# Table signs by memset, one filter copy and one evacuation moved to ScalarE, in the opening of an FFT filter + MLP kernel

## The chip, the cores and the metric

One core of a Trainium2 chip. The metric is device microseconds of one execution. A profiled execution leaves a trace; its "span" is 1.8 us shorter than the device time of the same execution (770.64 against 772.45 in the kernel before). Below, "us N" is an instant of a trace, counted from the start of its span. Instants with two decimals that stand in no fence are single records of a trace.

## The reference, cut to what matters

```python
def _attn_ref(x, filt_r, filt_i):            # x (8, 3008, 256)
    X = np.fft.rfft(x, axis=1)
    Y = X * (filt_r + 1j * filt_i)[None]
    return np.fft.irfft(Y, n=x.shape[1], axis=1)

def _moe_ref(x, w_in, w_out):                # (24064, 256) -> 2048 -> 256
    h = x @ w_in
    g = 0.5 * h * (1.0 + erf(h / sqrt(2)))
    return g @ w_out
```

The transform runs along 3008 = 47 x 64 as matmuls with tables: stage 1 over 47, a transpose, stage 2 over 64, the product with the filter, stages 3 and 4 back. The result of batch 0 feeds the first MLP matmul; from then on the kernel works on the MLP of one batch and the transform of the next side by side.

Of the kernel before, what the change touches and what calls it, by code (L numbers as in the profile page):

```python
# [10 lines left out]
ALU = mybir.AluOpType  # L11
FP32 = mybir.dt.float32
BF16 = mybir.dt.bfloat16
# [4 lines left out]
NA, NB = 47, 64  # L18
# [11 lines left out]
class _Mix:  # L30
# [63 lines left out]
    def dup_filters(self, eng, k0, k):  # L94
        for k in range(k0, k0 + k, 2):
            o, i = (self.F[r:r + 64, :, k:k + 2, :].rearrange("p t a b -> p t (a b)") for r in (64, 0))
            eng.tensor_copy(out=o, in_=i)  # L97

    def gate(self, t):

# [24 lines left out]
    def table_1(self, g):  # L125

        nc, ts = self.nc, self.nc.vector.tensor_scalar
        col = lambda name: g.tile([128, 1], FP32, name=name)
        off = g.tile([128, 2, K1], FP32, name="off")
        nc.vector.memset(off[:, 0, :], 0.25)  # L130
        nc.vector.memset(off[:, 1, :], 0.5)
        h, n1, hs, hc = col("h"), col("n1"), col("hs"), col("hc")
        ts(out=h, in0=self.p, scalar1=float(NA), scalar2=None, op0=ALU.is_ge)
        nc.vector.scalar_tensor_tensor(out=n1, in0=h, scalar=-float(NA), in1=self.p, op0=ALU.mult, op1=ALU.add)
        ts(out=hs, in0=h, scalar1=2.0 * PI, scalar2=None, op0=ALU.mult)
        ts(out=n1, in0=n1, scalar1=1.0 / NA, scalar2=None, op0=ALU.mult)
        ts(out=hc, in0=h, scalar1=-2.0 * PI, scalar2=2.0 * PI, op0=ALU.mult, op1=ALU.add)
        self.turn_signs(g)
        self.weights_4(g)
        w, r = g.tile([128, 2, K1], FP32, name="w1"), g.tile([128, 2, K1], FP32, name="r1")  # L140
        nc.vector.scalar_tensor_tensor(out=w, in0=self.k48, scalar=n1, in1=off, op0=ALU.mult, op1=ALU.add)
        ts(out=r, in0=w, scalar1=RND, scalar2=-RND, op0=ALU.add, op1=ALU.add)
        nc.vector.tensor_tensor(out=w, in0=w, in1=r, op=ALU.subtract)
        for q, s in enumerate((hc, hs)):
            nc.scalar.activation(out=self.T1[:, 48 * q:48 * q + 48], in_=w[0:2 * NA].rearrange("p a b -> p (a b)"),
                                 func=AF.Sin, scale=s[0:2 * NA])
# [16 lines left out]
    def table_2_angle(self, g, h):  # L163


        v = self.nc.vector
        ts = v.tensor_scalar
        w = self.gen[:, 0]
        if h == 0:
            col = lambda name: g.tile([128, 1], FP32, name=name)  # L170
            jn = g.tile([128, NB], FP32, name="jn")
            ts(out=jn, in0=self.jj, scalar1=self.n2, scalar2=self.ri, op0=ALU.mult, op1=ALU.add)
            n6, self.n12 = col("n6"), col("n12")
            ts(out=n6, in0=self.n2, scalar1=6.0, scalar2=None, op0=ALU.mult)
            ts(out=self.n12, in0=self.n2, scalar1=12.0, scalar2=None, op0=ALU.mult)
            v.scalar_tensor_tensor(out=w[:, 0:6], in0=self.kk.unsqueeze(2).to_broadcast([128, 6, NB]), scalar=self.n2,
                                   in1=jn.unsqueeze(1).to_broadcast([128, 6, NB]), op0=ALU.mult, op1=ALU.add)
            ts(out=w[:, 6:12], in0=w[:, 0:6], scalar1=n6, scalar2=None, op0=ALU.add)
        else:
            ts(out=w[:, 12:24], in0=w[:, 0:12], scalar1=self.n12, scalar2=None, op0=ALU.add)  # L180
        k = slice(12 * h, 12 * h + 12)
        ts(out=self.gen[:, 1, k].bitcast(I32), in0=w[:, k].bitcast(I32), scalar1=15, scalar2=None,
           op0=ALU.logical_shift_left)

    def turn_signs(self, g):

        ts = self.nc.vector.tensor_scalar
        q, b = (g.tile([128, 1], FP32, name=n) for n in ("q64", "b32"))
        self.turn = [g.tile([128, 1], FP32, name=n) for n in ("turn_r", "turn_i")]
        ts(out=q, in0=self.p, scalar1=64.0, scalar2=-64.0, op0=ALU.is_ge, op1=ALU.mult)  # L190
        self.nc.vector.tensor_tensor(out=q, in0=self.p, in1=q, op=ALU.add)
        ts(out=b, in0=q, scalar1=32.0, scalar2=2.0, op0=ALU.is_ge, op1=ALU.mult)
        ts(out=self.turn[0], in0=b, scalar1=1.0, scalar2=-1.0, op0=ALU.mult, op1=ALU.add)
        ts(out=self.turn[1], in0=b, scalar1=-1.0, scalar2=1.0, op0=ALU.mult, op1=ALU.add)

    def unit_matrices(self, g, cols):
        ts = self.nc.vector.tensor_scalar
# [13 lines left out]
    def table_2_swap(self, h):  # L211
        t2 = self.T2[:, 12 * h:12 * h + 12]
        for i in range(2):
# [2 lines left out]
                                  start=True, stop=True)  # L216
            self._evac(t2[:, :, 1, 32 * i:32 * i + 32], ps[:, 0:384].rearrange("p (k j) -> p k j", k=12),
                       "act", 1.0 - 2.0 * i)

    def weights_4(self, g):  # L220

        ts = self.nc.vector.tensor_scalar
        q, self.wt, self.wtc = (g.tile([128, 1], FP32, name=n) for n in ("q48", "wt", "wtc"))
        ts(out=q, in0=self.p, scalar1=48.0, scalar2=-48.0, op0=ALU.is_ge, op1=ALU.mult)
        self.nc.vector.tensor_tensor(out=q, in0=self.p, in1=q, op=ALU.add)
        ts(out=self.wt, in0=q, scalar1=2.0, scalar2=1.0, op0=ALU.is_ge, op1=ALU.add)
        ts(out=self.wtc, in0=self.p, scalar1=4.0, scalar2=1.0, op0=ALU.is_ge, op1=ALU.add)


    def table_4(self, t4, t1, wt, tag, eng):  # L230
# [297 lines left out]
def kernel(  # L528
# [9 lines left out]
    m = _Mix(ctx, tc, x, filt_r, filt_i, moe_w_in, moe_w_out, out)  # L538
    nc, B, S = tc.nc, m.B, m.S
# [3 lines left out]
    g = m.small  # L543
    wide = ctx.enter_context(ExitStack())
    m.psum(wide, w=(2, 1), m=(1, 1), n=(5, 1))
    act = "act"
# [7 lines left out]
    for sgn, lo, base in ((1, 0, 0), (-1, 32, m.S - NA)):  # L554
# [5 lines left out]
    m.ones = g.tile([128, 512], BF16, name="ones")  # L560
    nc.vector.memset(m.ones, 1.0)
    m.warm_up(10)
    m.table_1(g)
    m.table_2_rows(g)
    m.T1c = g.tile([2 * NA, 96], BF16, name="T1c")
    nc.vector.tensor_copy(out=m.T1c.rearrange("p (k h r) -> p k h r", h=2, r=2),
                          in_=m.T1.rearrange("p (h r k) -> p k h r", h=2, r=2))
    m.gen = m.py.tile([128, 2, K1, NB], FP32, tag="y", name="gen")
    m.table_2_angle(g, 0)
    m.unit_matrices(g, cols)  # L570
# [11 lines left out]
    for u in range(16):  # L582
# [12 lines left out]
        if u == 11:  # L595
# [2 lines left out]
            m.table_3_turn(0)  # L598
            m.warm_up(1)
    m.table_3(1)  # L600
    m.table_3_copy(1, False)
    m.dup_filters(nc.vector, 0, 4)
    m.warm_up(1)
    m.c1t(0, (False, False))
    m.c1t(1, (act,))
# [29 lines left out]
    m.load_x(1)  # L635
    m.load_w_out(0)
    m.load_w_out(8)

    warm = g.tile([128, 1], FP32, name="warm")
    nc.scalar.activation(out=warm, in_=m.p, func=AF.Gelu)  # L640
# [3 lines left out]
    for u in range(10):  # L644
        if u < 8:
            m.c3t(u)
        if u >= 2:
            m.c4(u - 2, (act, False if u > 7 else act))
    wide.close()
    m.psum(ctx, h=(3, 1), o=(2, 1), f=(3, 1))  # L650

# [29 lines left out]
    for s in range((NT + 1) * 16):  # L681
        t, jc = s // 16, s % 16
# [37 lines left out]
```

## The kernel before: the parts that the change touches

All of the change lies in "the opening": tables and the transform of batch 0, before the first MLP matmul.

```python
def dup_filters(self, eng, k0, k):           # second half of a filter tile: partitions 0..63 -> 64..127
    for k in range(k0, k0 + k, 2):
        o, i = (self.F[r:r + 64, :, k:k + 2, :].rearrange("p t a b -> p t (a b)") for r in (64, 0))
        eng.tensor_copy(out=o, in_=i)        # 64x1024, bf16

def table_3_turn(self, q):                   # two bf16 copies with a sign per partition, SBUF to SBUF
    k = slice(8 * q, 8 * q + 8)
    for r in range(2):
        self.nc.vector.tensor_scalar(out=self.T3i[:, k, r, :], in0=self.T3[:, k, 1 - r, :],
                                     scalar1=self.turn[r], scalar2=None, op0=ALU.mult)

def c2(self, p):                             # stage 2, and the product with the filter
    ...                                      # two matmuls into ps
    nc.vector.tensor_tensor(out=w, in0=ps.unsqueeze(1).to_broadcast([128, 2, 512]),
                            in1=f.rearrange("p t a b -> p t (a b)"), op=ALU.mult)
...
# ---- the body (cut) ----
m.table_1(g)
m.table_2_rows(g)
...
m.table_2_angle(g, 0)                        # begins with turn_signs and weights_4: nine 128x1 operations
...
for k, n in ((0, 4), (4, 8), (12, 12)):
    m.load_filters(k, n)                     # three groups of transfers, issued by Pool
m.load_w_in()
...
m.dup_filters(nc.gpsimd, 4, 20)              # ten copies on Pool
m.table_2_sin(0)
for u in range(16):
    m.c1(...)                                # stage 1; every four need another piece of x
    ...
m.table_3(1)
m.table_3_copy(1, False)                     # ScalarE
m.dup_filters(nc.vector, 0, 4)               # two copies on VectorE
m.warm_up(1)
m.c1t(0, (False, False))                     # transposes, evacuated to b_sb by VectorE
m.c1t(1, (act,))
m.c2(0)                                      # first product
m.table_3_turn(1)
m.warm_up(1)
m.c2(1)                                      # second product
...
for q in range(1, 7):
    if q < 6:
        m.c2(2 * q); ...; m.c2(2 * q + 1)    # third to twelfth product
    ...                                      # stage 3
for u in range(10):
    if u < 8:
        m.c3t(u)
    if u >= 2:
        m.c4(u - 2, (act, False if u > 7 else act))   # stage 4; False is VectorE
```

## Time and profile before

| | before |
|---|---|
| time, three runs | 772.91 us (772.91 to 772.94) |
| span of the profiled run | 770.64 us |
| first MLP matmul | 38.76 us |
| from there to the end of the span | 731.88 us |

The prediction below shows the lines of this profile and reads them.

### The profile page before, as it was taken

What the parts mean: (1) busy time and instruction counts of PE and PEld (TensorE: products, weight loads), DVE (VectorE), ACT (ScalarE), POOL (GpSimd) and SP (SyncE); (2) the same over time, 40 slices, a digit from 0 to 9 for tenths busy, and PEclk for the clock granted to TensorE, in tenths of its full rate; (3) what the DMA queues carried; (4) which work ended last, traced back from release to release, by engine and by line L of the source; (5) the groups of instructions that cost most, each with busy time, mean ns of one, the idle gap of its engine ahead of it and who ended that gap; (6) DMA issues with size and microseconds to landing.
All of it is one profiled execution on the core that took longest, in us unless ns stands there. A gap on an engine that the chain in (4) does not pass through costs nothing.

```text
span 770.6 us, 15044 instructions
## 1 busy us (share of the span) xinstructions
PE 763.5 (99%) x6057; PEld 527.5 (68%) x6057; DVE 398.5 (52%) x737; ACT 566.7 (74%) x977; POOL 62.5 (8%) x154
## 2 busy tenths in 40 slices
PE   8999999999999999999999999999999999999998
PEld 5857666776766766677777777667676777766666
DVE  8957755564545645466463664627646366411011
ACT  6879855897568975699656996579865798666663
POOL 7701100010000200011000110001100000000000
PEclk9999999999999999999999999999999999999999
DMA  9884645366163661636526364345553422410111
GB/s 153 150 197 115 136 125 129 115 138 155 40 173 88 128 158 47 187 79 125 138 58 176 85 133 124 83 151 105 114 137 84 136 83 70 123 42 28 42 42 55
DMA packets 87270, 85.66 MB, mean 111 GB/s; under 512 B 6688, under 2 KB 77472, under 8 KB 87200
## 3 DMA queue, kind: packets, MB, share of 16 engines
q1 hardware_dynamic: 78816, 68.70, 31.3%
q0 software_dynamic: 8384, 16.00, 14.1%
q8 instruction: 47, 0.77, 0.4%
q14 instruction: 23, 0.19, 0.1%
HBM read 54.00 MB, written 46.66 MB: 131 GB/s over the span
## 4 chain that ended last, share of the span: by engine, by line
PE 94%; DMA 3%; POOL 2%; issue 0%; DVE 0%; POOLq 0%; SPq 0%
PE ps_o L509 43%; PE ps_h L482 42%; PE ps_s L369 2%; PE ps_s L344 2%; PE ps_s L319 2%; PE ps_s L296 2%; DMA x_sb<-in_x_dram 2%; POOL x_sb L83 1%; DMA F<-in_filt_i_dram 1%; POOL F L97 1%; DMA d_sb<-R 0%; POOL F L92 0%; PE ps_e L499 0%; POOL T1s L282 0%; DVE ost L522 0%
## 5 line engine op out<-in xcount | busy, mean ns | idle before, releaser
L485 ACT ACTIVATE g_sb<-ps_h 128x512 bf16<-128x512 f32 x752 | 438.0, 597 | 183.4 <-PE ps_h L482 172.6
L509 PE MATMUL ps_o<-w_out_sb,g_sb 128*128 128x256 bf16 x2992 | 447.5, 273 | 0.0
L482 PE MATMUL ps_h<-y_sb,w_in_sb 128*128 128x512 bf16 (+3 forms) x1600 | 445.8, 366 | 0.7 <-DMA x_sb<-in_x_dram 0.7
L509 PEld LDWEIGHTS <-g_sb 128*128 128x128 bf16 x2992 | 283.9, 98 | 134.3 <-issue 9.9
L482 PEld LDWEIGHTS <-w_in_sb 128*128 128x128 bf16 x1600 | 154.7, 98 | 23.7 <-issue 1.1
L515 DVE COPY ost<-ps_o 128x512 f32<-128x512 f32 x93 | 63.8, 686 | 143.5 <-PE ps_o L509 143.4
L327 DVE TENSOR_TENSOR p<-ps_s,F 128x512 bf16<-128x512 f32 x84 | 58.1, 692 | 105.8 <-ACT p L326 89.4
L273 DVE TENSOR_SCALAR y_sb<-ps_s 128x376 bf16<-128x376 f32 x112 | 61.0, 548 | 80.7 <-PE ps_s L369 80.7
L271 DVE CAST a_sb<-ps_s 128x512 bf16<-128x512 f32 x112 | 69.4, 683 | 27.7 <-PE ps_s L296 27.7
L271 DVE CAST v_sb<-ps_s 128x512 bf16<-128x512 f32 x84 | 57.4, 685 | 2.9 <-PE ps_s L344 2.9
L325 ACT ACTIVATE p<-ps_s 64x512 bf16<-64x512 f32 x84 | 49.8, 593 | 2.0
L326 ACT CAST p<-ps_s 64x512 bf16<-64x512 f32 x84 | 48.5, 577 | 1.0
L369 PEld LDWEIGHTS <-d_sb 96*128 96x128 bf16 x448 | 30.7, 97 | 25.6 <-DMA d_sb<-R 0.6
L102 POOL COPY gate<-p 1x1 bf16<-1x1 bf16 x48 | 8.5, 176 | 470.7 <-DVE p L329 470.7
L329 DVE TENSOR_TENSOR p<-p 128x512 bf16<-128x512 bf16 x84 | 35.7, 425 | 2.9
L369 PE MATMUL ps_s<-T,d_sb 96*128 96x94 bf16 x448 | 36.3, 204 | 0.1
L328 DVE TENSOR_TENSOR p<-p,F 128x512 bf16<-128x512 bf16 x84 | 34.9, 415 | 0.0
L83 POOL DMA_DIRECT2D x_sb<-in_x_dram x64 | 32.6, 511 | 13.3 <-issue 12.8
L344 PE MATMUL ps_s<-p,T 128*128 128x256 bf16 x168 | 32.1, 273 | 0.0
L319 PE MATMUL ps_s<-b_sb,T 128*128 128x256 bf16 x168 | 32.1, 273 | 0.0
L344 PEld LDWEIGHTS <-T 128*128 128x128 bf16 x168 | 16.4, 98 | 20.1 <-DVE p L329 0.5
L319 PEld LDWEIGHTS <-T 128*128 128x128 bf16 x168 | 16.4, 98 | 13.4
(113 smaller groups left out, 195.0 us busy)
## 6 DMA issues: line engine op xcount, KB each, us to landing
out_dram<-ost SPq DMA_DIRECT2D x93, 256.0 KB, 2.4
x_sb<-in_x_dram POOLq DMA_DIRECT2D x64, 188.0 KB, 3.6
R<-a_sb SPq DMA_DIRECT2D x112, 96.0 KB, 2.1
b_sb<-R SPq DMA_DIRECT2D x28, 384.0 KB, 4.1
R<-v_sb SPq DMA_DIRECT2D x42, 256.0 KB, 3.3
d_sb<-R SPq DMA_DIRECT2D x56, 192.0 KB, 4.7
w_in_sb<-in_moe_w_in_dram POOLq DMA_DIRECT2D x2, 512.0 KB, 9.0
w_out_sb<-in_moe_w_out_dram POOLq DMA_DIRECT2D x2, 512.0 KB, 11.0
```

Source lines behind the costliest of these rows:

```text
L271: self.nc.vector.tensor_copy(out=out, in_=in_)
L273: self.nc.vector.tensor_scalar(out=out, in0=in_, scalar1=scale, scalar2=None, op0=ALU.mult)
L319: nc.tensor.matmul(ps[:, 256 * i:256 * i + 256], lhsT=self.T2[:, k].rearrange("p a b -> p (a b)"), rhs=self.st[b, "b", k // 6][:, k % 6, : ...
L325: nc.scalar.activation(out=p2[0:64], in_=ps[64:128], func=AF.Copy, scale=-1.0)
L326: nc.scalar.copy(out=p2[64:128], in_=ps[0:64])
L327: nc.vector.tensor_tensor(out=p1, in0=ps, in1=f(0), op=ALU.mult)
L344: nc.tensor.matmul(ps[:, 256 * i:256 * i + 256], lhsT=self.T3[:, k].rearrange("p a b -> p (a b)"), rhs=w[:, 256 * i:256 * i + 256], start= ...
L369: nc.tensor.matmul(ps[:, 94 * i:94 * i + 94], lhsT=d[:, (grp % 2) * 4 + i, 128 * half:128 * half + 128], rhs=t4, start=True, stop=True)
L482: nc.tensor.matmul(ps[:, o:o + n], lhsT=self.w_in_sb[:, dc, jc * 128:jc * 128 + 128], rhs=self.ring[:, dc, off:off + n], start=(dc == 0), ...
L485: nc.scalar.activation(out=self.st["g", t][:, jc, :], in_=ps, func=AF.Gelu)
L509: nc.tensor.matmul(ps[:, tile_i % 2, :], lhsT=g[:, jc, tile_i * 128:tile_i * 128 + 128], rhs=self.w_out_sb[:, jc, :], start=(jc == 0), sto ...
L515: nc.vector.tensor_copy(out=ost, in_=ps)
```

## The change

Its intent is a shorter opening. (1) Sign columns that were computed from the partition's number are set by memsets; weights that only later batches need go to Pool, behind the opening's work; the tables that the sine waits for are computed earlier. (2) Of the two filter copies that stand on VectorE ahead of the first product, one goes to ScalarE. (3) The last evacuation of stage 4 goes from VectorE to ScalarE.

```diff
     def dup_filters(self, eng, k0, k):
-            eng.tensor_copy(out=o, in_=i)
+            (eng.copy if eng is self.nc.scalar else eng.tensor_copy)(out=o, in_=i)
 ...                                   # (1) in table_2_angle
-        self.turn_signs(g)             # five operations of VectorE
-        self.weights_4(g)              # four operations of VectorE
+        self.table_2_rows(g)
 ...                                   # T1c moves into the middle of the angles
+    def signs(self, g):                # called ahead of table_1
+        for t, s in zip(self.turn, (-1.0, 1.0)):
+            set_(t, s)                 # memset
+            for lo in (32, 96):
+                set_(t[lo:lo + 32], -s)
+        set_(self.wtc, 2.0)
+        set_(self.wtc[0:4], 1.0)
+    def weights_4(self, g):            # now three operations of Pool, called behind load_w_out
 ...                                   # (2)
     m.table_3(1)
+    m.dup_filters(nc.scalar, 0, 2)
     m.table_3_copy(1, False)
-    m.dup_filters(nc.vector, 0, 4)
+    m.dup_filters(nc.vector, 2, 2)
 ...                                   # (3)
-            m.c4(u - 2, (act, False if u > 7 else act))
+            m.c4(u - 2, (False if u > 7 else act, act))
```

More of the change, by code (lines that the diff above doesn't have):

```diff
@@ L177, in table_2_angle @@
                                    in1=jn.unsqueeze(1).to_broadcast([128, 6, NB]), op0=ALU.mult, op1=ALU.add)
+            self.T1c = g.tile([2 * NA, 96], BF16, name="T1c")
+            v.tensor_copy(out=self.T1c.rearrange("p (k h r) -> p k h r", h=2, r=2),
+                          in_=self.T1.rearrange("p (h r k) -> p k h r", h=2, r=2))
             ts(out=w[:, 6:12], in0=w[:, 0:6], scalar1=n6, scalar2=None, op0=ALU.add)
@@ L183, in table_2_angle @@
            op0=ALU.logical_shift_left)
-    def turn_signs(self, g):
-        ts = self.nc.vector.tensor_scalar
-        q, b = (g.tile([128, 1], FP32, name=n) for n in ("q64", "b32"))
+    def signs(self, g):
+        set_ = self.nc.vector.memset
         self.turn = [g.tile([128, 1], FP32, name=n) for n in ("turn_r", "turn_i")]
-        ts(out=q, in0=self.p, scalar1=64.0, scalar2=-64.0, op0=ALU.is_ge, op1=ALU.mult)
-        self.nc.vector.tensor_tensor(out=q, in0=self.p, in1=q, op=ALU.add)
-        ts(out=b, in0=q, scalar1=32.0, scalar2=2.0, op0=ALU.is_ge, op1=ALU.mult)
-        ts(out=self.turn[0], in0=b, scalar1=1.0, scalar2=-1.0, op0=ALU.mult, op1=ALU.add)
-        ts(out=self.turn[1], in0=b, scalar1=-1.0, scalar2=1.0, op0=ALU.mult, op1=ALU.add)
+        for t, s in zip(self.turn, (-1.0, 1.0)):
+            set_(t, s)
+            for lo in (32, 96):
+                set_(t[lo:lo + 32], -s)
+        self.wtc = g.tile([128, 1], FP32, name="wtc")
+        set_(self.wtc, 2.0)
+        set_(self.wtc[0:4], 1.0)
+    def weights_4(self, g):
+        ts = self.nc.gpsimd.tensor_scalar
+        q, self.wt = (g.tile([128, 1], FP32, name=n) for n in ("q48", "wt"))
+        ts(out=q, in0=self.p, scalar1=48.0, scalar2=-48.0, op0=ALU.is_ge, op1=ALU.mult)
+        self.nc.gpsimd.tensor_tensor(out=q, in0=self.p, in1=q, op=ALU.add)
+        ts(out=self.wt, in0=q, scalar1=2.0, scalar2=1.0, op0=ALU.is_ge, op1=ALU.add)
     def unit_matrices(self, g, cols):
@@ L218, in table_2_swap @@
                        "act", 1.0 - 2.0 * i)
-    def weights_4(self, g):
-        ts = self.nc.vector.tensor_scalar
-        q, self.wt, self.wtc = (g.tile([128, 1], FP32, name=n) for n in ("q48", "wt", "wtc"))
-        ts(out=q, in0=self.p, scalar1=48.0, scalar2=-48.0, op0=ALU.is_ge, op1=ALU.mult)
-        self.nc.vector.tensor_tensor(out=q, in0=self.p, in1=q, op=ALU.add)
-        ts(out=self.wt, in0=q, scalar1=2.0, scalar2=1.0, op0=ALU.is_ge, op1=ALU.add)
-        ts(out=self.wtc, in0=self.p, scalar1=4.0, scalar2=1.0, op0=ALU.is_ge, op1=ALU.add)
     def table_4(self, t4, t1, wt, tag, eng):
@@ L562 @@
     m.warm_up(10)
+    m.signs(g)
     m.table_1(g)
-    m.table_2_rows(g)
-    m.T1c = g.tile([2 * NA, 96], BF16, name="T1c")
-    nc.vector.tensor_copy(out=m.T1c.rearrange("p (k h r) -> p k h r", h=2, r=2),
-                          in_=m.T1.rearrange("p (h r k) -> p k h r", h=2, r=2))
     m.gen = m.py.tile([128, 2, K1, NB], FP32, tag="y", name="gen")
@@ L637 @@
     m.load_w_out(8)
+    m.weights_4(g)
     warm = g.tile([128, 1], FP32, name="warm")
```

## The prediction

> **What bounds the kernel now.** I read the page first (busy time by engine), then busy time by stretch, then the chain that ended last, then the timeline of the first 60 us instruction by instruction. All edits lie before the first MLP matmul at 38.76 us.
>
> ```profile
> PE 763.5 (99%) x6057; PEld 527.5 (68%) x6057; DVE 398.5 (52%) x737; ACT 566.7 (74%) x977; POOL 62.5 (8%) x154
> ...
> core 0: us, PE busy (x) PEld busy (x) DVE busy (x) ACT busy (x) POOL busy (x), PEclk, DMA share, GB/s
> ...
> 12.50:18.60 6.10, 5.52 (x68) 3.98 (x69) 5.90 (x13) 5.00 (x8) 5.42 (x10) 1.00 1.20 180
> 18.60:31.00 12.40, 12.09 (x151) 9.79 (x151) 11.90 (x13) 10.75 (x20) 12.22 (x19) 1.00 0.72 131
> ...
> 38.75:765.90 727.15, 727.02 (x5604) 500.36 (x5605) 362.87 (x653) 536.52 (x921) 32.79 (x96) 1.00 0.44 109
> ```
> From 38.75 us on TensorE idles 0.13 us in 727.15 (727.15 - 727.02). So the change is worth exactly what it moves the instant 38.76, and that instant alone is to be predicted.
>
> ```profile
> 5.78 6.56 DMA x_sb<-in_x_dram
> 12.63 2.35 POOL F L92 x4
> ...
> 31.24 7.39 DMA x_sb<-in_x_dram
> 38.63 0.12 issue
> 38.76 0.59 PE ps_h L482 x2
> ```
> The chain names transfers of x. The first is real: x of batch 0 lands until 12.34. The second I don't believe: the built order shows that this weight load waits for VectorE and for one DMA lane, this matmul for ScalarE; the lane had what is needed (w_in) at 23.61, and the lane's next piece of x lands at 39.35, after the start. At 38.63 only parts of it arrive. VectorE's last evacuation ends at 38.61, so that is the releaser.
>
> ```profile
> 6.71 0.84 ACT L208 ACTIVATE T<-gen 128x768 bf16<-128x768 int32 x1 [2.28 <-DVE gen L182]
> 8.23 0.87 ACT L269 ACTIVATE T<-ps_sw 128x384 bf16<-128x384 f32 x2
> 8.61 0.72 PEld L385 LDWEIGHTS <-x_sb 94*128 94x128 bf16 x16 [0.64 <-issue]
> 12.45 0.72 PEld L385 LDWEIGHTS <-x_sb 94*128 94x128 bf16 x16 [0.41 <-issue]
> 13.81 1.02 ACT L269 ACTIVATE T<-ps_t 128x1024 bf16<-128x1024 bf16 x1
> 13.99 0.90 DVE L97 COPY F<-F 64x1024 bf16<-64x1024 bf16 x2
> 14.92 0.76 DVE L271 COPY b_sb<-ps_c1t 128x512 bf16<-128x512 bf16 x2
> ...
> 17.41 1.05 POOL L97 COPY F<-F 64x1024 bf16<-64x1024 bf16 x1 [0.55 <-DMA F<-in_filt_i_dram]
> ...
> 17.48 11.40 DVE L412 TENSOR_TENSOR p<-ps_c,F 128x1024 bf16<-128x1024 f32 x10
> ```
> To see: ScalarE waits 2.28 us for the sine angles; the four groups of stage-1 matmuls start 0.1 us after pieces of x land (records: 5.79, 8.50, 10.46, 12.35); then the copies of filters on VectorE stand ahead of b_sb; and from 17.48 VectorE multiplies without a gap, 1.13 us apart, while Pool makes the filter halves, 0.98 apart, from 17.41.
>
> ```profile
> 37.53 0.87 ACT L269 ACTIVATE y_sb<-ps_c 128x376 bf16<-128x376 f32 x2
> 38.06 0.55 DVE L273 TENSOR_SCALAR y_sb<-ps_c 128x376 bf16<-128x376 f32 x1 [0.22 <-PE ps_c L459]
> 38.72 0.13 PEld L482 LDWEIGHTS <-w_in_sb 128*128 128x128 bf16 x2 [0.85 <-DMA x_sb<-in_x_dram]
> 38.76 0.59 PE L482 MATMUL ps_h<-y_sb,w_in_sb 128*128 128x512 bf16 x2 [0.73 <-DMA x_sb<-in_x_dram]
> ```
> To see: the last evacuation is VectorE's, 0.55 us, and weight load plus matmul follow it by 0.11 and 0.15 us.
>
> **What the Trainium skill says.** "ScalarE: Activation LUTs", section "What ACT_TABLE_LOAD costs": an ACTIVATE with immediates takes 186 ns + 0.833 ns per element, neighbours overlapping by about 93 ns. For 1024 elements 1039, trace 1023; for 376 elements 499, trace 478 to 505: agrees. "VectorE: DVE Perf Modes", "The perf-mode tier table": bf16 copies inside SBUF run four elements a cycle; the second filter copy took 405 ns for 1024 elements, which one a cycle could not: agrees. "TensorE: Matmul & The Clock Gate", "What's actually happening": TensorE starts at half clock until about 3.4 us of activity. The trace has warm-up matmuls 0.43 us apart until 5.27 and 0.22 apart from 7.44: agrees, the switch coming later; it matters as TensorE itself holds the start below. "Perfetto Trace Analysis", "Optimizing Scalar/DVE Operations": Pool and VectorE share a read port, so moving work between them might not help. The weights moved to Pool are three tiny operations where Pool is idle (34.07 to 66.56 in the timeline); no conflict to expect.
>
> **Part 1, sign columns and order of tables.** Removed from VectorE ahead of the angles: nine 128x1 operations, 1.865 to 3.06 = 1.20 us. Added ahead: eight memsets. Two independent memsets start 0.03 us apart here, a dependent one about 0.11 later; five steps of 0.03 and three of 0.11 are 0.48 us. The six row operations (0.5 us) now come before the phase w and no longer after it, so w comes 0.2 us earlier (1.20 - 0.48 - 0.5), and jn starts when Pool's iota jj is there, 3.69 instead of 4.62. Its chain then ends about 0.92 earlier, with T1c sunk into the wait between two angle operations: sine at about 5.79 instead of 6.71. What it is worth: ScalarE's next dependence on TensorE is the swap product at 8.23. TensorE gets there by its own queue: stage 1 starts when x lands (5.79; ten warm-ups also issue until then), 16 matmuls at 0.08, three warm-ups, swap at 7.87, where the sine was already ready at 7.55. Then x lands at 8.50. So ScalarE and VectorE get idle time near 7.6 and 9.8 to 10.9, and the next groups stay at 8.61, 10.57, 12.45. Worth 0.00 us.
>
> **Part 2, one filter copy on ScalarE.** VectorE's evacuation of at_sb ends at 13.96 as before. Without the second copy b_sb could start at 14.49, but its eight transposes end at 14.63: start 14.66 instead of 14.92, 0.26 earlier. The product that follows moves from 15.82 to 15.56, the second from 17.48 to 17.22, the third from 18.61 to 18.35, if the filter half is there. It is not: Pool's first copy starts on a landing at 17.25 and ends at 18.46, so the third starts at 18.50. Gain 0.11 us, kept by the rest of the run since Pool's pace (0.98) is faster than VectorE's (1.13). ScalarE pays: its T3 copy goes from 13.81 to about 14.7, b_sb(1) from 15.12-16.14 to 15.6-16.65. Its user, the third product's matmul, waits anyway for a PSUM bank until 16.8, so 0.15 us of slack is left there, and over a microsecond before VectorE needs the result. All that follows until 37.3 hangs on VectorE or TensorE and moves by the same 0.11.
>
> **Part 3, last evacuation on ScalarE.** The last product is done at 38.02, held by a bank that ScalarE frees at 37.64: unchanged. ScalarE, free by then (38.02), starts at 38.06 and takes 0.48 instead of 0.55: ends 38.54. VectorE's last now ends about 38.30, so the weight load is out of the way, and the matmul follows ScalarE by 0.05 (as the matmul at 37.69 follows 37.64) and not by 0.15: start 38.59 instead of 38.76. Gain 0.16.
>
> **Weights on Pool**: wt is used at 53.3, ready by 35: 0.
>
> **Sum**: 0.00 + 0.11 + 0.16 = 0.27, 772.91 - 0.27 = 772.64 us.
>
> **Rivals.** (a) The whole 0.92 us of part 1 comes through: 771.7. For it: ScalarE works almost without a gap from 6.71 to 14.83. Against: within that stretch TensorE's groups follow landings of x by 0.1 us. (b) Part 2 backfires: ScalarE's added copy, 1.0 us, delays T3 and b_sb(1) until they bind: if the matmul waits, up to 0.9 later, 773.5. Against: over 1 us of slack there. (c) Filters land at another time, or Pool's copies are the true pace: part 2 gives 0 to 0.26, so 772.8 to 772.5. (d) The chain is right and x of batch 1 holds 38.76: then part 3 gives nothing and part 2 neither, 772.9. Against: the landing of 39.35.
>
> **Range and chances.** The parts give 0 to 0.45 us; another build can shift landings by some tenths, and the three runs of before differ by 0.03. So 772.64, from 772.1 to 773.0. Two per cent are 15.5 us, 40% of the whole opening: faster 0.003, slower 0.004, same 0.993.
>
> **What would show it.** Sine near 5.8 but stage-1 groups still at 8.6, 10.6, 12.45 and ScalarE idle ahead of 8.23 (part 1). The third product near 18.50, directly behind Pool's first copy, and b_sb near 14.66 (part 2). A ScalarE evacuation last, 38.4 in all, and the first MLP matmul at about 38.49, that is 38.76 less the sum, with 727.2 us from there to 765.9 less the sum. Wrong if stage 1's later groups moved with the sine, if c2 waited for b_sb(1), or if the first MLP matmul moved by more than 0.5 us or later.

## The result, and the profile after

| | before | after |
|---|---|---|
| six timed runs each (three of before are those above) | 772.91 us (772.22 to 773.18) | 773.05 us (772.55 to 773.66) |
| ratio after/before | | 1.0003, 95% interval 0.999 to 1.0016: same |
| span of the profiled run | 770.64 us | 770.78 us |
| first MLP matmul | 38.76 us | 38.78 us |
| from there to the end of the span | 731.88 us | 732.00 us |

The ratio is the mean time of one kernel's fast runs over that of the other's, so not quite the ratio of the medians. The outputs are right. The time is the same, as the chances had it; but the median lies 0.05 us above the range given (772.1 to 773.0), and the 0.27 us gained by the sum are not there. About a hundred matmul records of line 486 are missing from the trace after, so TensorE's busy time isn't compared.

Timeline of the kernel after, its opening, the lines between these left out (columns: start us, duration us, engine, line, operation, output <- input, shapes, count, and in brackets the idle time just before and what ended it):

```profile
5.89 0.84 ACT L221 ACTIVATE T<-gen 128x768 bf16<-128x768 int32 x1 [1.43 <-DVE gen L185]
7.88 0.87 ACT L273 ACTIVATE T<-ps_sw 128x384 bf16<-128x384 f32 x2 [0.38 <-PE ps_sw L228]
12.27 0.72 PEld L389 LDWEIGHTS <-x_sb 94*128 94x128 bf16 x16 [0.38 <-issue]
13.74 1.05 ACT L97 COPY F<-F 64x1024 bf16<-64x1024 bf16 x1
14.52 0.76 DVE L275 COPY b_sb<-ps_c1t 128x512 bf16<-128x512 bf16 x2
15.49 1.22 DVE L416 TENSOR_TENSOR p<-ps_c,F 128x1024 bf16<-128x1024 f32 x1 [0.21 <-PE ps_c L412]
17.15 1.21 DVE L416 TENSOR_TENSOR p<-ps_c,F 128x1024 bf16<-128x1024 f32 x1
17.47 3.98 POOL L97 COPY F<-F 64x1024 bf16<-64x1024 bf16 x4 [0.97 <-DMA F<-in_filt_i_dram]
18.54 4.62 DVE L416 TENSOR_TENSOR p<-ps_c,F 128x1024 bf16<-128x1024 f32 x4 [0.17 <-POOL F L97]
```

To see: the sine starts 0.82 us earlier than before (6.71), and nothing is gained by it: ScalarE now idles ahead of the swap at 7.88, and the last group of stage 1 follows the landing of x (12.17 here, 12.35 before) by 0.10 us as it did. ScalarE takes one filter copy (13.74). The third product, at 18.54, now waits for Pool's first copy; before, it stood at 18.61 in an unbroken row of VectorE. So 0.07 us are won here.

The same, a few us on (Pool's fifth filter copy, then the seventh product, 0.18 us later than before, where it stood at 23.14):

```profile
22.25 2.02 POOL L97 COPY F<-F 64x1024 bf16<-64x1024 bf16 x2 [0.80 <-DMA F<-in_filt_i_dram]
...
23.32 1.23 DVE L416 TENSOR_TENSOR p<-ps_c,F 128x1024 bf16<-128x1024 f32 x1 [0.17 <-POOL F L97]
```

To see: Pool idles 0.80 us for the last filter transfer. It landed at 22.11 here and at 21.18 in the trace before, where Pool wanted it at 21.36. The chain of waits of the kernel before had this transfer in it, in lines that the prediction cut away (start us, us, what):

```profile
14.98 6.20 DMA F<-in_filt_i_dram
...
21.36 0.18 POOL F L97
...
22.34 4.97 POOL F L97 x5
```

To see: in the trace before, too, the last filter was only just there: it landed 0.18 us ahead of Pool's fifth copy, and where Pool waits for a filter its copy starts 0.14 to 0.16 us behind the landing (22.11 to 22.25 in the trace after). VectorE had more room: that copy ended at 22.40 and the seventh product, which needs it, started at 23.14. So, as an estimate, the last filter could have landed 0.75 us later (0.04 for Pool, 0.71 for VectorE) before a product waited. In the trace after it landed 0.93 us later, and VectorE's row stood 0.07 us earlier: 0.25 us of waiting.

The end of the opening of the kernel after, timeline first, then its chain of waits:

```profile
38.59 0.29 PEld L486 LDWEIGHTS <-w_in_sb 128*128 128x128 bf16 x2 [0.53 <-DMA x_sb<-in_x_dram]
38.78 0.38 PE L486 MATMUL ps_h<-y_sb,w_in_sb 128*128 128x512 bf16 x1 [0.57 <-ACT y_sb L273]
```

```profile
37.55 0.67 PE ps_c L463 x8
38.24 0.49 ACT y_sb L273
```

To see: TensorE's idle time ahead of the first MLP matmul is 0.57 us (0.73 before), and the chain now goes through ScalarE's evacuation, no longer through a transfer of x.

From the end of the last product to the first MLP matmul it was 8.68 us before (30.08 to 38.76) and is 8.52 after (30.26 to 38.78). The balance of the two traces is therefore: -0.07 at the third product, +0.25 by the wait for the last filter (which makes +0.18 at the seventh), -0.16 at the end: +0.02 at the first MLP matmul. From there to the end the two differ by 0.12.

### The profile page after: what moved, and what is told of

It reads as the page before. It is cut to its first block, busy times and chain, and to the rows that moved or that the text cites. A ratio compares the mean times of both kernels' runs of the same rounds, so it can differ in the third digit from the quotient of the medians.

```text
span 770.8 us, 14944 instructions
## 1 busy us (share of the span) xinstructions
PE 756.9 (98%) x5953; PEld 527.0 (68%) x6057; DVE 397.3 (52%) x735; ACT 567.9 (74%) x978; POOL 63.4 (8%) x157
## 4 chain that ended last, share of the span: by engine, by line
PE 95%; DVE 1%; DMA 1%; issue 1%; ACT 1%; POOL 0%; DVEq 0%; POOLq 0%; SPq 0%
PE ps_o L513 43%; PE ps_h L486 39%; PE ps_s L348 3%; PE ps_s L373 3%; PE ps_s L323 2%; PE ps_s L300 2%; DMA x_sb<-in_x_dram 1%; PE ps_c L434 1%; DVE p L416 1%; PE ps_c3t L449 0%; DMA d_sb<-R 0%; PE ps_c L412 0%; POOL x_sb L83 0%; PE ps_c L463 0%; PE ps_e L503 0%
## 5 line engine op out<-in xcount | busy, mean ns | idle before, releaser
L486 PE MATMUL ps_h<-y_sb,w_in_sb 128*128 128x512 bf16 (+3 forms) x1500 | 424.5, 365 | 0.6 <-ACT y_sb L273 0.6
```

Of the source, the lines that this page charges most:

```text
L486: nc.tensor.matmul(ps[:, o:o + n], lhsT=self.w_in_sb[:, dc, jc * 128:jc * 128 + 128], rhs=self.ring[:, dc, off:off + n], start=(dc == 0), ...
```

## The experiments

The theories, by the letters that the expectations use: (L) the moved parts do what was reckoned, and landings of transfers, which differ from run to run, hide the sum; (C) the change itself delays the filter transfers, from e9 on (C2) ScalarE's filter copy does. The rival in e1: x of batch 1 holds the first MLP matmul, so that the end of stage 4 gains nothing. Another, (P), came from the runs themselves: a short copy of VectorE collides with Pool's filter copies. "T3i copies" are the turn copies of `table_3_turn`.

This table collects every trace. "x" is the landing of the last piece of x of batch 0, "F2" and "F3" the landings of the second and the last group of filters, "turn" the start and the duration in ns of the second of the two copies of `table_3_turn(1)`; then the starts of the third and seventh product, the end of the last, the first MLP matmul, and from there to the end of the span. The letters say which parts are in.

| trace | parts | x | F2 | F3 | turn | 3rd | 7th | end | MLP | rest |
|---|---|---|---|---|---|---|---|---|---|---|
| before | - | 12.35 | 17.25 | 21.18 | 17.22, 349 | 18.61 | 23.14 | 30.08 | 38.76 | 731.88 |
| e8 before again | - | 12.36 | 17.30 | 21.52 | 17.33, 345 | 18.72 | 23.25 | 30.18 | 38.85 | 731.67 |
| e12 before again | - | 12.85 | 17.41 | 22.29 | 17.72, 1129 | 19.90 | 24.42 | 31.35 | 40.03 | 732.13 |
| e15 before again | - | 11.97 | 17.11 | 21.36 | 17.10, 349 | 18.50 | 23.02 | 29.95 | 38.63 | 732.06 |
| after | 123 | 12.17 | 17.31 | 22.11 | 16.89, 346 | 18.54 | 23.32 | 30.26 | 38.78 | 732.00 |
| e4 after again | 123 | 12.29 | 16.94 | 22.52 | 17.10, 1186 | 19.34 | 23.86 | 30.79 | 39.30 | 732.19 |
| e11 after again | 123 | 12.22 | 17.94 | 22.28 | 17.01, 345 | 19.17 | 23.70 | 30.63 | 39.15 | 731.99 |
| e16 after again | 123 | 12.54 | 17.85 | 22.55 | 17.26, 346 | 19.08 | 23.76 | 30.71 | 39.22 | 731.79 |
| e1 | 3 | 12.24 | 17.45 | 21.97 | 17.15, 348 | 18.68 | 23.21 | 30.14 | 38.66 | 731.72 |
| e2 | 2 | 11.96 | 17.01 | 22.24 | 17.20, 1155 | 19.41 | 23.93 | 30.86 | 39.54 | 731.87 |
| e3 | 1 | 12.78 | 18.00 | 22.14 | 17.54, 346 | 19.23 | 23.76 | 30.69 | 39.37 | 731.98 |
| e9 | 1, 3 | 12.85 | 17.82 | 22.69 | 17.72, 345 | 19.11 | 23.91 | 30.85 | 39.36 | 731.72 |
| e10 | 1, 3, turn first | 12.51 | 17.41 | 22.12 | 16.09, 434 | 18.70 | 23.34 | 30.28 | 38.80 | 731.93 |
| e5 | 123, turn first | 12.80 | 17.84 | 23.05 | 16.05, 491 | 19.07 | 24.26 | 31.21 | 39.72 | 732.03 |
| e6 | 123, turn late | 11.92 | 16.74 | 21.51 | 18.02, 1127 | 19.07 | 23.59 | 30.51 | 39.03 | 731.80 |
| e7 | e5, w_in late | 12.36 | 16.79 | 22.25 | 15.70, 334 | 18.22 | 23.47 | 30.93 | 39.45 | 735.28 |
| e13 | 2 doubled | 12.32 | 17.40 | 21.79 | 17.33, 346 | 18.73 | 23.31 | 30.26 | 38.94 | 731.67 |
| e14 | 2 doubled | 12.45 | 17.27 | 22.36 | 17.36, 346 | 18.75 | 23.57 | 30.52 | 39.20 | 731.81 |

The repeats of one kernel ran on different chips (before: e8, e12 and e15 on chips 5, 14 and 10; after: e4, e11 and e16 on 4, 14 and 10), so their differences mix chip and execution. One kernel twice on one chip is e13 and e14 alone; there F2 differs by 0.13 us and F3 by 0.57.

Times, in us, each against the kernel before in the same rounds (e1 to e4 in one set, e5 to e7 in another, e9 and e10 in a third, each set on one chip; five runs of each kernel, six of e7, nine to eleven of the kernel before):

| run | median | before | ratio, 95% |
|---|---|---|---|
| e1 | 772.99 | 772.66 | 1.0003, 0.999 to 1.0015 |
| e2 | 773.20 | 772.66 | 1.0004, 0.9991 to 1.0017 |
| e3 | 772.41 | 772.66 | 0.9999, 0.9986 to 1.0011 |
| e4 | 772.43 | 772.66 | 0.9996, 0.9982 to 1.0009 |
| e5 | 772.78 | 773.11 | 0.9994, 0.9981 to 1.0007 |
| e6 | 773.31 | 773.11 | 1.0001, 0.9989 to 1.0013 |
| e7 | 774.11 | 773.11 | 1.0019, 1.0007 to 1.0031 |
| e9 | 772.49 | 772.40 | 1.0001, 0.9988 to 1.0015 |
| e10 | 772.39 | 772.40 | 0.9999, 0.9987 to 1.0012 |

### e1: part 3 alone

```diff
-            m.c4(u - 2, (act, False if u > 7 else act))
+            m.c4(u - 2, (False if u > 7 else act, act))
```

> Kernel before plus part 3 alone. Theory L (the last filter transfer, which lands some tenths to a microsecond earlier or later from execution to execution, decides when Pool can go on with its copies, and eats what part 2 gains): part 3 is independent of it, so the first MLP matmul follows the last product of stage 4 by 0.58 us and not by 0.74 us; 0.16 us off the time, which the spread of single executions (about 0.5 us) may hide. Theory C (the change itself delays the filters): filters land as in the trace before, the last at about 21.2 us. Rival (x of batch 1 holds the first MLP matmul): that distance stays 0.74 us.

Timeline, the first MLP matmul:

```profile
38.66 0.38 PE L482 MATMUL ps_h<-y_sb,w_in_sb 128*128 128x512 bf16 x1 [0.57 <-ACT y_sb L269]
```

Product end to first MLP matmul: 8.52 us. The rival falls. Every trace with part 3 (ten of them) has 8.51 or 8.52, every trace without it (eight) 8.67 or 8.68, whenever x of batch 1 came: the 0.16 us are part 3's, and VectorE's evacuation was what held the matmul before. The time shows nothing of it: 0.16 us are 0.0002 of the whole, the interval is six times as wide on either side.

### e2: part 2 alone

```diff
     m.table_3(1)
+    m.dup_filters(nc.scalar, 0, 2)
     m.table_3_copy(1, False)
-    m.dup_filters(nc.vector, 0, 4)
+    m.dup_filters(nc.vector, 2, 2)
```

> Kernel before plus part 2 alone. Theory L: third product directly behind Pool's first copy, and if the last filter transfer lands by about 21.2 us the product chain ends 0.11 us earlier than in the trace before (last product's second half done at 29.97 and not 30.08 us); with each 0.1 us that it lands later than 21.2 us the seventh product comes up to 0.1 us later. Theory C: if part 2 is what delays filters, the last lands near 22.1 us again as in the changed kernel.

Not as any theory had it: the second of VectorE's two turn copies took 1155 ns in place of 349, so the second product started at 18.28 (17.48 before) and the first MLP matmul at 39.54. Pool's first filter copy had started at 17.17, just ahead of it. That is where theory P comes from. The first product shows a smaller thing: it now waits for two engines (TensorE, for its matmul, and ScalarE, for the filter copy), VectorE has an extra semaphore instruction ahead of it, and the product starts 0.107 us behind its matmul's end where it was 0.037 in traces without part 2 (all records; e10, with the turn copies in between, apart). So of the 0.26 us by which the first product was to come earlier, 0.07 stay with that wait.

### e3: part 1 alone

The edit is the first part of the diff above, without (2) and (3).

> Kernel before plus part 1 (signs by memsets, order of tables, weights on Pool) alone. Both theories: sine at about 5.9 us and not 6.7 us, groups of stage 1 still 0.1 us behind landings of x, so 0.00 us of gain; ScalarE idle ahead of the swap's evacuation. Theory C: if the earlier table work is what delays the filters (VectorE working while Pool makes descriptors), the last one lands near 22.1 us; theory L: anywhere from 21 to 22 us.

The sine started at 5.91 us, the first MLP matmul at 39.37, for x and the filters landed 0.4 and 0.75 us later than in the trace before; the distance from the end of the products is the old 8.68. Part 1 is worth nothing, as predicted, and adds no work to the path.

### e4: the kernel after, again

> The changed kernel once more, unedited. Theory L: last filter transfer at another time than 22.11 us, and the first MLP matmul follows it: if it lands at 21.2 us or earlier the first MLP matmul is near 38.5 us. Theory C: 22.1 us again, first MLP matmul near 38.78 us.

The same program as the trace after, and the first MLP matmul came 0.52 us later. Here it is the collision again (VectorE, then Pool, in the timeline):

```profile
17.10 1.19 DVE L260 TENSOR_SCALAR T3i<-T,turn_i 128x512 bf16<-128x512 bf16 x1
```

```profile
17.10 2.08 POOL L97 COPY F<-F 64x1024 bf16<-64x1024 bf16 x2 [0.40 <-DMA F<-in_filt_i_dram]
```

Pool's first copy took 1033 ns and ended at 18.13, VectorE's ended at 18.28. The copy shows as a long instruction, not as a wait.

### e5 and e6: the turn copies ahead of, and inside, Pool's copies

e5: VectorE's turn copies go ahead of the first product (and ScalarE's T3 copy ahead of its filter copy, so that they can).

```diff
+    m.table_3_copy(1, False)
     m.dup_filters(nc.scalar, 0, 2)
-    m.table_3_copy(1, False)
 ...
+    m.table_3_turn(1)
     m.c2(0)
-    m.table_3_turn(1)
```

> The changed kernel with the T3i copies of VectorE moved ahead of the first product, and ScalarE's T3 copy ahead of its filter copy. Theory P (in e2 and e4 the second T3i copy took 1.16 and 1.19 us and not 0.35, ending right after a Pool filter copy that had begun within 0.03 us of it: the two engines exclude each other, and the order depends on when the filters land): T3i now ends near 16 us, a microsecond before the filters land, so both T3i copies take 0.35 us in every execution and the product chain isn't delayed by them; third product directly behind Pool's first copy; mean time 0.2 to 0.4 us below the changed kernel's and less spread. Theory L (only the last filter transfer counts): no difference from the changed kernel, as the seventh product still waits for it when it lands late.

e6: they go behind the second product, where Pool is sure to be copying.

```diff
-    m.table_3_turn(1)
     m.warm_up(1)
     m.c2(1)
+    m.table_3_turn(1)
     m.c1t(2, (act,))
```

> The changed kernel with the T3i copies moved behind the second product, so that they always fall into Pool's run of filter copies. Theory P: at least one T3i copy takes about as long as Pool's copy still has to run (up to 1.2 us and not 0.35), in every execution; third product 0.5 to 1.5 us later than 18.54 us, time 0.4 to 1.3 us longer than the changed kernel's. Without exclusion: both take 0.35 us, third product at about 18.5 us, no change in time.

Timeline of e6, VectorE, then Pool:

```profile
17.76 0.34 DVE L260 TENSOR_SCALAR T3i<-T,turn_r 128x512 bf16<-128x512 bf16 x1
18.02 1.13 DVE L260 TENSOR_SCALAR T3i<-T,turn_i 128x512 bf16<-128x512 bf16 x1
```

```profile
16.90 3.13 POOL L97 COPY F<-F 64x1024 bf16<-64x1024 bf16 x3 [0.65 <-DMA F<-in_filt_i_dram]
```

The slow copy can be forced: inside Pool's row of copies one of the two took 1127 ns, ended 0.15 us behind the Pool copy beside it (19.144 against 18.993), and the third product started at 19.07, though the second group of filters had landed earlier than in any other trace (16.74). In e5 the turn copies were done before the filters landed, and took 345 and 491 ns. P is shown. It isn't the whole cost: in e5 the filters landed at 17.84 and 23.05, and the first MLP matmul stood at 39.72 without any collision. In time both are the same as before; the forecasts of time for e5 and e6 were against the changed kernel, which was not run in these rounds, so they stay unchecked.

### e7: e5, with w_in loaded later

Whether w_in, issued behind the filters, is what delays the last filter.

```diff
-    m.load_w_in()
 ...
-    m.dup_filters(nc.gpsimd, 4, 20)
+    m.dup_filters(nc.gpsimd, 4, 16)
+    m.load_w_in()
+    m.dup_filters(nc.gpsimd, 20, 4)
```

> As e5, and the load of w_in is issued behind Pool's eighth filter copy and not ahead of the first. Theory L and P together: the last filter transfer no longer shares the DMA engines with w_in and lands before 21.5 us, so Pool's fifth copy starts without a wait, products run 1.13 us apart from the third on, and the first MLP matmul comes at about 38.3 to 38.5 us; mean time 0.3 to 0.6 us below the changed kernel's. If the filters' landing doesn't depend on w_in: last transfer at 21.2 to 22.5 us as before, same as e5.

It is not, by this one trace: the last filter landed at 22.25 all the same. And the kernel lost, 1.0019 with an interval clear of 1. (The profiled execution is the slowest of its six, 776.51 us against a median of 774.11, so the 3 us below are not its usual loss.) The first MLP matmul stood at 39.45; the loss comes behind it, where the rest is 735.28 us against 731.67 to 732.19 elsewhere. Its chain of waits shows on what:

```profile
42.40 5.79 DMA R<-a_sb
...
48.27 2.10 DMA R<-a_sb
```

w_in, landing at 33.96 (27.45 in e5), pushed x of batch 1 (last piece 43.4 us; 42.3 in e5), w_out (50.7; 48.3 in e5) and with them the stores of stage 1; VectorE waited 2.21 us for these (0.71 in e5) and TensorE 1.53 us for VectorE. That is about half of the loss: behind this idle time the granted clock of TensorE was 0.50 from 51.24 to 54.66 us, where e5 had 1.00. As an estimate, half of these 3.42 us, 1.71, is lost by it; with 1.53 that makes the 3.25 us between the rests of e7 and e5. A transfer of 1 MB (w_in is two of 512 KB) that is needed later isn't free to move into later traffic.

### e8, e11: before and after once more

> The kernel before once more, unedited, for a second trace. Theory P: the kernel before runs the same risk; if the filters of the second group land before about 17.05 us its second T3i copy takes about 1.2 us, else 0.35. Theory C (the change makes the landings late): last filter at about 21.2 us again; theory L: anywhere from 21 to 22.5 us.

> The changed kernel, third trace. Theory C2: the last filter transfer 4.8 us or more behind the second group's; theory L: anywhere from 3.9 to 5.6. Theory P: if the second T3i copy starts within 0.1 us before or later than Pool's first filter copy it takes over 1 us, else 0.35. End of products to first MLP matmul 8.52 us.

e8 gave 38.85, near the trace before. The order of the two copies was the other here (VectorE, then Pool, lines of the timeline):

```profile
17.33 0.34 DVE L256 TENSOR_SCALAR T3i<-T,turn_i 128x512 bf16<-128x512 bf16 x1
```

```profile
17.46 1.10 POOL L97 COPY F<-F 64x1024 bf16<-64x1024 bf16 x1 [0.50 <-DMA F<-in_filt_i_dram]
```

VectorE's copy started first, and now Pool's is the longer one (1104 ns; 1032 to 1035 in the traces where it ran alone). e11 gave 39.15: no collision, but filters at 17.94, so that the third product waited for Pool until 19.17.

### e9, e10: without part 2, and with the turn copies first

e9 is the kernel after with both filter copies on VectorE again. e10 is e9 with the turn copies ahead of the first product.

```diff
+    m.table_3_turn(1)
     m.c2(0)
-    m.table_3_turn(1)
```

> The changed kernel without part 2 (both filter copies on VectorE again). In the six traces so far with part 2 the last filter transfer lands 4.8 to 5.6 us behind the last of the second group, in the four without it 3.9 to 4.5 us. Theory C2 (ScalarE's filter copy, or what it moves, delays the transfers): here 3.9 to 4.6 us again. Theory L (chance of the transfers alone): anywhere from 3.9 to 5.6 us. Both: last stage-1 product to first MLP matmul shortened by part 3, so that the first MLP matmul is 8.52 us behind the end of the products.

> As e9, with the T3i copies ahead of the first product. Theory P: T3i ends before 16.3 us, ahead of any landing of the second filter group (16.7 to 18.0 us so far), so no T3i copy waits for Pool's filter copies; the third product still starts directly behind Pool's first copy or at about 18.6 us; first MLP matmul at 38.5 to 38.9 us, depending on the landings. Theory C2: landing distance 3.9 to 4.6 us.

Timeline of e10, VectorE:

```profile
15.83 0.35 DVE L260 TENSOR_SCALAR T3i<-T,turn_r 128x512 bf16<-128x512 bf16 x1
16.09 0.43 DVE L260 TENSOR_SCALAR T3i<-T,turn_i 128x512 bf16<-128x512 bf16 x1
16.44 3.46 DVE L416 TENSOR_TENSOR p<-ps_c,F 128x1024 bf16<-128x1024 f32 x3
```

The turn copies are out of the way, and the products run back to back, 1.13 us apart, beside Pool's copies (one of their inputs lies in PSUM; the products of 1024 elements took 1.20 to 1.23 us in every trace). The first MLP matmul stood at 38.80, inside the 38.5 to 38.9 forecast. e10 has the lowest median of the tried kernels, 772.39 us against 772.40 of before in the same rounds: the same. In both the last filter (22.69, 22.12) held Pool's fifth copy and the seventh product, without ScalarE's filter copy: so that wait is not part 2's alone.

### e12 to e16: is the late last filter part 2's doing?

Left open by then: with part 2 the last filter tended to land later behind the second group. e12 and e15 are the kernel before, e16 the kernel after; e13 and e14 double the suspected cause in the kernel before.

```diff
+    m.dup_filters(nc.scalar, 0, 4)
     m.table_3_copy(1, False)
-    m.dup_filters(nc.vector, 0, 4)
```

> The kernel before, third trace. Theory C2: the last filter transfer 3.9 to 4.6 us behind the second group's; theory L: anywhere from 3.9 to 5.6. Theory P as for the changed kernel. End of products to first MLP matmul 8.68 us.

> Kernel before with both first filter copies on ScalarE (double the dose of part 2). If ScalarE's copying delays the filters' transfers: last transfer 5.3 us or more behind the second group's, later than 22.5 us. If landings are chance: 3.9 to 5.6 us behind, 21.2 to 22.7 us.

> The same kernel again, for a second trace: delay theory 5.3 us or more, chance 3.9 to 5.6 us.

> The kernel before, fourth trace, on the same chip as e13 and e14: delay theory 3.9 to 4.9 us behind the second group's, chance 3.9 to 5.6 us.

> The changed kernel, fourth trace, on the same chip: delay theory 4.7 to 5.6 us behind the second group's, chance 3.9 to 5.6 us.

From the second group's landing to the last (F3 less F2): without part 2 3.93 to 4.88, mean of eight traces 4.44; with part 2 4.34 to 5.58, mean of eight 5.01; with two copies on ScalarE 4.39 and 5.09. The forecasts of C2 failed in e9, e10, e11 and e12 and in both traces of the double dose, which isn't longer than the single one. But C2 isn't refuted. Counted from the landing of the last piece of x (column "x"), the last filter came 8.83 to 9.84 us later without part 2 (mean 9.42) and 9.59 to 10.28 with it (mean 10.03), and on each chip every trace with part 2 lies above every one without; the double dose lies between (9.47, 9.91). The second group, all issued before ScalarE's copy starts, shows no such shift (means 4.98 and 5.02). So a shift of about 0.6 us by part 2 is likely, but it was looked for after the runs, and what in the copy should do it isn't shown. By the same count part 2 lost rather than gained: from the landing of x to the seventh product it was 10.79 to 11.06 us in the seven traces without part 2 and without a collision, and 11.11 to 11.97 in all eight with part 2.

Between e12 and e15, the same program on two chips, the first MLP matmul moved by 1.40 us (40.03 and 38.63). e12 shows that the collision needs no part of the change (VectorE, then Pool):

```profile
17.46 0.34 DVE L256 TENSOR_SCALAR T3i<-T,turn_r 128x512 bf16<-128x512 bf16 x1
17.72 1.13 DVE L256 TENSOR_SCALAR T3i<-T,turn_i 128x512 bf16<-128x512 bf16 x1
18.77 1.21 DVE L412 TENSOR_TENSOR p<-ps_c,F 128x1024 bf16<-128x1024 f32 x1
```

```profile
17.57 2.17 POOL L97 COPY F<-F 64x1024 bf16<-64x1024 bf16 x2 [0.21 <-DMA F<-in_filt_i_dram]
```

To see: between two starts of VectorE, 17.72 and 18.77, lies a copy that takes 0.35 us otherwise. The second product started at 18.77, in the trace before at 17.48.

## Why the prediction was right or wrong

- **Only the first MLP matmul counts: right.** Over 17 traces (all but e7) that instant ranges over 1.40 us, and the rest from there over 0.52 (731.67 to 732.19).
- **Part 1 worth 0.00: right.** Sine at 5.89 (5.79 predicted; the eight memsets took 0.79 us by the records and not 0.48), stage 1 behind the landings of x, ScalarE idle ahead of the swap. Shown by the trace after and e3.
- **Part 3 worth 0.16: right, to the hundredth.** Shown by 18 traces. With it rival (d) falls.
- **Part 2 worth 0.11, "kept by the rest of the run since Pool's pace (0.98) is faster than VectorE's (1.13)": this is the step that failed.** b_sb came 0.71 us behind the end of at_sb (0.70 predicted). The third product directly behind Pool's first copy came true too, as 18.54 (18.50 predicted): a gain of 0.07 in place of 0.11. But the gain was not kept. Pool's pace is its own only while its input is there; its fifth copy needs the last filter transfer, which landed 0.93 us later than in the trace before, where about 0.75 could be spared. The seventh product lost 0.25 us against the third, and the sum became +0.02 in place of -0.27: by the prediction's own sign, "or later", wrong. How much of the 0.93 is part 2's doing and how much chance is open (e12 to e16). The profile before had it: the transfer stood in the chain of waits, in lines that the prediction left out and did not ask after. As an estimate: with a last filter at 21.18 us and no wait, the trace after would have kept the 0.07, and the first MLP matmul would have come at 38.76 - 0.07 - 0.16 = 38.53. In the repeats of the kernel after, other inputs of the same row struck: the collision in e4, the late second group in e11 (17.94) and e16 (17.85), and in e16 the last filter for another 0.15 us.
- **The 0.11 itself took one landing for a constant.** The third product starts 1.23 us behind the second group's landing when it waits for Pool (17.31 to 18.54, 17.94 to 19.17, 17.85 to 19.08). Before, VectorE's own row brought it to 18.50 to 18.72. So part 2 can gain only if the filters land before about 17.4 (18.6 less 1.23, an estimate), and in the four traces of the kernel after they landed at 16.94, 17.31, 17.85 and 17.94. In the first of these the collision took 0.8 us. That leaves one in four. Rival (c) named the landing, with 0 as its worst; the worst is a loss. Rival (b), that part 2 backfires, named ScalarE's own later copies, which did not bind.
- **"No conflict to expect" on the shared port: right for the tiny weights, and asked of the wrong operations.** The Trainium skill, "SBUF — State Buffer", section "🔬 SBUF: two separate sides", says that VectorE (in a 2-port perf mode, or with two inputs from SBUF against a GpSimd instruction that reads SBUF) and GpSimd take a shared port pair as "an exclusive lock, not a bandwidth split", a whole instruction at a time, whichever starts first. The traces agree, though none tells which mode the turn copy ran in: 1127 to 1186 ns in place of 345 to 349 for the turn copy when Pool started first (e2, e6, e12) or within 3 ns of it (e4), and up to 1172 (e14, by the records) in place of 1033 for Pool's copy when VectorE did. Since it also struck the kernel before (e12), it isn't a cost of the change; but it makes an earlier landing of filters worse than a slightly later one.
- **The range, 772.1 to 773.0: too narrow.** It rested on three runs that differ by 0.03 us. 35 fast executions of the kernel before, over four sets, run from 772.12 to 774.39 with a standard deviation of 0.45 and a mean of 772.78; the eleven fast ones of the kernel after have a mean of 772.82 and a deviation of 0.52. With 0.45, two means of six runs differ by 0.26 as one standard deviation (0.45 times the root of 2/6): the whole effect looked for is of the size of the noise, and the 0.14 us between the two medians is no loss that could be shown.
- **Chances: right**; nothing here is near 2%.

What stays open: why the landings of the filters differ by over a microsecond between traces, how much of it is the chip, and what in part 2 shifts the last one, if it does. No kernel tried beats the two beyond the noise.

## What to carry to other kernels

Before a gain on one engine is called kept, follow every later point at which another queue or a transfer has to catch up, and read its slack in the trace: a slack of 0.75 us in one trace is not enough when landings move by a microsecond. A gain of a few tenths is to be read from a distance between two events that no transfer stands between (8.68 to 8.52 here, in every trace), not from the time. And look for bf16 copies of VectorE that run beside copies of Pool: a start 0.1 us earlier or later made 0.35 us into 1.13.

## What the Trainium skill lacked or had wrong

- "SBUF — State Buffer", section "🔬 SBUF: two separate sides": agrees, but tells a delay for Pool's descriptor writing alone, and not how the lock looks in a profile of two copies. The blocked copy of VectorE shows no wait; it is one long instruction (1127 to 1186 ns in place of 345 to 349), ending 0.15 us after Pool's. The other way round, Pool's copy ended 0.89 to 0.90 us after VectorE's (the first copy in e8 and e14, 1104 and 1172 ns in place of 1033). Products of VectorE with an f32 input from PSUM kept 1.20 to 1.23 us beside Pool's copies.
- "Perfetto Trace Analysis", section "Identifying Dependency Chains": it says that an instruction which waits for several engines may have semaphore instructions put before it, but gives no cost. Here the second semaphore cost the product behind its matmul 0.07 us (0.107 against 0.037).
- No page gives the spread of DMA landings for one program: the last filter transfer landed between 21.18 and 22.29 us in the four traces of the kernel before, and between 22.11 and 22.55 in those of the kernel after (over several chips), and held the seventh product by 0.25 us in one of the latter and 0.15 in another.
